# Talking-heads attention and squared-ReLU FFN: pairs of heads transposed at full width, and one stock of PSUM banks

## The chip, the cores and the metric

The kernel runs on one core of one Trainium2 chip. The metric is the device time of one execution in microseconds. TensorE (PE) multiplies matrices into PSUM, which has eight banks; VectorE (DVE) and ScalarE (ACT) read PSUM and write SBUF; GpSimd (POOL) works on SBUF and issues DMAs, SyncE (SP) issues DMAs.

## What is computed

The reference, cut to its core (8 batches, 12 heads, 448 positions, head size 64; the FFN is 768 to 2048 to 768):

```python
scores = scale * np.matmul(q, k.transpose(0, 1, 3, 2))
scores = np.einsum('bhij,hg->bgij', scores, w_pre)
scores = scores - np.max(scores, axis=-1, keepdims=True)
attn = np.exp(scores)
attn = attn / (np.sum(attn, axis=-1, keepdims=True) + 1e-09)
attn = np.einsum('bhij,hg->bgij', attn, w_post)
x = np.matmul(attn, v)            # heads side by side: [8*448, 768]
h = np.maximum(x @ w_in, 0.0)
out = (h * h) @ w_out
```

The heads are mixed before and after the softmax, so all twelve heads of a query row are needed together.

## The kernel before

**Attention, per batch.** q and k of a batch lie in SBUF as bf16, positions in partitions (`qs`, `ks`). For each of the six pairs of heads, `t_qk` transposes both heads' q and k on TensorE into one PSUM bank (a product with the identity `ident` as the moving operand): for each of 4 row groups of q and 4 blocks of k, and for each head of the pair, one product of 64 stationary columns that writes PSUM partitions 0 to 63 or 64 to 127. These are lines L274 (q) and L279 (k), 16 products per pair. Three copies bring the result out: `kt` takes both heads' k in one copy of 128 partitions, `qz` takes each head's q into its own half, with zeros in the other half, so that a score product over 128 partitions gives one head. `qz` and `kt` have 8 slots, so a pair's transposes wait for the last scores of the pair that had the slot before.

`score` (L312) multiplies one head and 112 query rows by 448 keys; an eviction copies it to `snat`, of which there are two. When the 12 heads of a row group are there, DMAs on SyncE's queue (`relayout`, L335) rearrange `snat` into 11 chunks `sch`, each with 10 query rows by 12 heads in 120 partitions. `chunk` then does, 45 times per batch: the mix product m (L365), a minimum on VectorE (L370; signs are turned), the exponential on ScalarE (L373), a reciprocal on VectorE (L379), the second mix's weights on GpSimd (`wq`, L382), four products that transpose and mix at once (L389), and an eviction to `atb`. `av` (L434) multiplies by v with products of 64 columns, evicted on ScalarE (L443) to `xt`.

**FFN.** `unit` works on 128 or 256 positions of a pair of batches: L478 multiplies by the first weights, ScalarE applies the ReLU (L491), GpSimd squares (L494), L510 multiplies by the second weights, VectorE evicts (L525), SyncE stores.

**What sets the order.** TensorE, VectorE, ScalarE and GpSimd run in the order that `Planner.run` writes out. Every operation has an engine (or VectorE and ScalarE, either of them), a cost in ns, a priority (lower goes first, in chunks: chunk c of batch b is 45b + c), the operations that it waits for, and possibly a bank that it takes or gives back. The planner plays time forward; when an engine is idle it takes the most urgent operation that is ready, even one meant for far later. FFN operations have priorities from a million on, so they fill what attention leaves. `copy` is the helper that makes an eviction on VectorE (L233) or ScalarE (L235).

**Banks.** The eight PSUM banks are four pairs with a tag: m for the mix product, a for L389, f for the FFN, g for transposes, scores and av. In the first row group of the first batch scores go round all four tags, and every second transpose of that batch uses f. An operation that needs a bank waits in the plan until its own tag has one free.

**Loads.** The loads of the next batch's q and k are issued by GpSimd at steps 3 and 6 of a batch (18 and 21 in the first), in two groups of three pairs; they wait for that step's `wq` (`gate`) and for the transposes that read the old contents.

Of the kernel before, what the change touches and what calls it, by code (L numbers as in the profile page):

```python
# [23 lines left out]
NR = 4  # L24
PR = S // NR
# [7 lines left out]
NB = 4  # L33
W2B = 2 * S
NSLOT = 8
NE = 5
NSCH = 8
AHEAD = 5
UNITS = [(0, 128), (128, 384), (384, 640), (640, 896)]


# [11 lines left out]
class Planner:  # L53
# [2 lines left out]

    def __init__(self):
        self.ops = []
        self.banks = {}

    def add(self, eng, ns, pri, fn, deps=(), lat=60, bank=None, frees=None):
        op = Op(eng if isinstance(eng, dict) else {eng: ns}, lat, pri, fn, list(deps), bank, frees)
        self.ops.append(op)
        return op

    def run(self):
        order, events, n = [], [], 0
        ready, busy, held = {}, {}, {}
        free = {tag: list(slots) for tag, slots in self.banks.items()}

        def push(op):
            nonlocal n
            for eng in op.engs:
                heapq.heappush(ready.setdefault(eng, []), (op.pri, n, op))
            n += 1

        for op in self.ops:
            for eng in op.engs:
                busy.setdefault(eng, 0)
                ready.setdefault(eng, [])  # L80
            if op.left == 0:
                push(op)
        t = 0
        while True:
            for eng, heap in ready.items():
                if busy[eng] > t:
                    continue
                kept = []
                while heap:
                    item = heapq.heappop(heap)  # L90
                    op = item[2]
                    if op.eng is not None:
                        continue
                    if op.bank is not None and not free[op.bank[0]]:
                        kept.append(item)
                        continue
                    args = []
                    if op.bank is not None:
                        held[op.bank] = free[op.bank[0]].pop(0)
                        args.append(held[op.bank])  # L100
                    if len(op.engs) > 1:
                        args.append(eng)
                    op.eng, op.ns, op.at = eng, op.engs[eng], t
                    order.append((op, args))
                    busy[eng] = t + op.ns
                    heapq.heappush(events, (t + op.ns, n, None))
                    heapq.heappush(events, (t + op.ns + op.lat, n + 1, op))
                    n += 2
                    break
                for item in kept:  # L110
                    heapq.heappush(heap, item)
            if not events:
                break
            t = events[0][0]
            while events and events[0][0] == t:
                op = heapq.heappop(events)[2]
                if op is None:
                    continue
                if op.frees is not None:
                    free[op.frees[0]].append(held.pop(op.frees))  # L120
                for x in op.next:
                    x.left -= 1
                    if x.left == 0:
                        push(x)
        assert len(order) == len(self.ops)
        return order
# [3 lines left out]
def kernel(  # L130
# [11 lines left out]
    nc = tc.nc  # L142
    P = nc.NUM_PARTITIONS

    sb = ctx.enter_context(tc.tile_pool(name="sb", bufs=1))
    ps = ctx.enter_context(tc.tile_pool(name="ps", bufs=1, space=bass.MemoryType.PSUM))

    def many(n, name, shape, dtype):
        return [sb.tile(shape, dtype, name=f"{name}{i}") for i in range(n)]
# [3 lines left out]
    vs = sb.tile([P, H, NB, D], BF16, name="vs")  # L153
    qz = many(NSLOT, "qz", [P, 2, S], BF16)
    kt = many(NSLOT, "kt", [P, S], BF16)
    snat = many(2, "snat", [PR, H, S], BF16)
    sch = many(NSCH, "sch", [KC, S], BF16)
    schl = many(2, "schl", [KC, S], BF16)
# [9 lines left out]
    osb = many(2, "osb", [P, DMODEL], F32)  # L168
    w1 = many(NPAIR, "w1", [P, DFF], BF16)
    w2 = many(FT, "w2", [P, DMODEL], BF16)  # L170
    bank = {tag: [ps.tile([P, 512], F32, name=f"{tag}{i}") for i in range(2)] for tag in "mafg"}

    def load_q(b, h0, h1):
        nc.gpsimd.dma_start(
# [56 lines left out]
    def copy(eng, out_, in_):  # L231
        if eng == "DVE":
            nc.vector.tensor_copy(out=out_, in_=in_)  # L233
        else:
            nc.scalar.copy(out=out_, in_=in_)  # L235

    pl = Planner()
    pl.banks = {tag: bank[tag] for tag in bank}
    add = pl.add
    FILL = 1e6  # L240
    slots = {}
# [1 line left out]
    def keep(key, fn):  # L243
        def go(slot):
            slots[key] = slot
            fn(slot)
        return go
# [15 lines left out]
    av_op, xc_op = {}, {}  # L263
    h_op, sq_op, o_op, st_op = {}, {}, {}, {}

    def t_qk(b, p):
        z, kk = qz[(b * NPAIR + p) % NSLOT], kt[(b * NPAIR + p) % NSLOT]
        key = ("f" if b == 0 and p % 2 else "g", "t", b, p)

        def mms(slot):  # L270
            v_ = slot[:, :].bitcast(BF16).rearrange("p (a c) -> p a c", a=2)
            for r in range(NR):
                for x in range(2):
                    nc.tensor.transpose(  # L274
                        v_[64 * x:64 * x + 64, 0, r * PR:(r + 1) * PR], qs[:, 2 * p + x, r, :], ident[0:PR, 0:PR],
                    )
            for j in range(NB):
                for x in range(2):
                    nc.tensor.transpose(  # L279
                        v_[64 * x:64 * x + 64, 1, j * 128:(j + 1) * 128], ks[:, 2 * p + x, j, :], ident[:, :],  # L280
                    )

        def part():
            return slots[key][:, :].bitcast(BF16).rearrange("p (a c) -> p a c", a=2)

        def out_k(eng):
            copy(eng, kk[:, :], part()[:, 1, 0:S])

        def out_q(x, eng):
            copy(eng, z[64 * x:64 * x + 64, x, :], part()[64 * x:64 * x + 64, 0, 0:S])  # L290

        pri = b * NCHUNK - 19 + 1.5 * p
        old = []
        i = b * NPAIR + p - NSLOT
        if i >= 0:
            old = [score_ops[i // NPAIR, NR - 1, 2 * (i % NPAIR) + x] for x in range(2)]
        mm = add("PE", 780, pri, keep(key, mms), [q_in[b, p // 2], k_in[b, p // 2]] + old, lat=200, bank=key)
        a0 = add({"DVE": 310, "ACT": 440}, 0, pri, out_k, [mm])
        a1 = add({"DVE": 390, "ACT": 440}, 0, pri, lambda eng: out_q(0, eng), [mm])
        a2 = add({"DVE": 390, "ACT": 440}, 0, pri, lambda eng: out_q(1, eng), [mm])  # L300
        add("FREE%d" % len(pl.ops), 0, pri, lambda: None, [a0, a1, a2], frees=key)
        trans[b, p] = (mm, [a0, a1, a2])
# [274 lines left out]
    for b in range(B):  # L577
# [10 lines left out]
        for r in range(NR):  # L588
            for h in range(H):
                score(b, r, h)  # L590
            for c in range(CPR * r, CPR * (r + 1)):
                relayout(b, c)
                chunk(b, c)
                n = n0 + c
                if b == 0 and c in (3, 6, 9):
                    load_w1(2 + c // 3, n, gate(n))
                if b == 0 and len(w2_in) < FT and (c in range(12, 18) or c >= 24):
                    ft = len(w2_in)
                    w2_in.append(load(3.9e5, n, lambda ft=ft: nc.gpsimd.dma_start(
                        out=w2[ft][:, :], in_=moe_w_out[ft * 128:(ft + 1) * 128, 0:DMODEL], max_dma_last_dim=1024,  # L600
                    ), gate(n)))
                if b + 1 < B and c in ((18, 21) if b == 0 else (3, 6)):
                    g0 = 0 if c in (3, 18) else 6
                    wars = [trans[b, p][0] for p in range(g0 // 2, g0 // 2 + 3)]
                    got = [
                        load(7e5, n, lambda b=b, g0=g0: load_q(b + 1, g0, g0 + 6), wars + gate(n)),
                        load(4e5, n, lambda b=b, g0=g0: load_lo(ks, k, b + 1, g0, g0 + 6), wars + gate(n)),
                        load(3e5, n, lambda b=b, g0=g0: load_hi(ks, k, b + 1, g0, g0 + 6), wars + gate(n)),
                    ]
                    both = add("DMA", 0, n, lambda: None, got, lat=0)  # L610
                    later[b + 1, g0] = both
            if r == 1:
                for g in range(3):
                    av(b, 0, g)
                if b > 0:
                    unit(b // 2, 0 if b % 2 == 0 else 2)
# [54 lines left out]
```

## Time and profile before

Three runs took 661.95, 665.9 and 667.5 us, the median is 665.9 us. The profiled execution took 667.06 us, and its span from first to last instruction is 665.3 us.

| | busy us | share of the span |
|---|---|---|
| TensorE products | 618.6 | 93% |
| TensorE weight loads | 444.9 | 67% |
| VectorE | 519.0 | 78% |
| ScalarE | 515.2 | 77% |
| GpSimd | 313.1 | 47% |

Busy time is the union of an engine's instructions. A product's record includes the depth of TensorE's pipeline, which the next product overlaps, so what a product occupies is read from the distance between starts. The granted TensorE clock is 0.969 of full speed over the span. Busy shares are averages over stages with different limits: the start-up (the first 100 us, when weights are loaded as well), six and a half batches of steady work, and an end with the FFN alone.

### The profile page before, as it was taken

The page shows a single profiled execution, that of the slowest core. Times are in us where ns is not written, and L with a number is a line of the kernel's source. Part 1 is how long each engine was busy: PE and PEld are TensorE (multiplying, and loading weights), DVE is VectorE, ACT ScalarE, POOL GpSimd, SP SyncE. Part 2 cuts the span into 40 slices and gives each one's busy share as a digit, 9 for nine tenths or more (in the row PEclk, how much of TensorE's full clock was granted, in tenths as well). Part 3 has the DMA queues.
Part 4 walks back from the last instruction along what each step waited for, and adds up shares of the span by engine and source line. Part 5 has one row for each costly group of instructions (what it writes and reads, how often), then busy time and mean ns, then how long its engine had stood idle before and what let it go on. Part 6 is the DMA issues. An engine that isn't in the chain of part 4 may idle for free.

```text
span 665.3 us, 17942 instructions
## 1 busy us (share of the span) xinstructions
PE 618.6 (93%) x6152; PEld 444.9 (67%) x6152; DVE 519.0 (78%) x1281; ACT 515.2 (77%) x1297; POOL 313.1 (47%) x570
## 2 busy tenths in 40 slices
PE   4778779999998999989999999999999999999996
PEld 2346537766766768766776777775776767777774
DVE  6688687899786897879979798779879798869511
ACT  3578777888876898888887888898888878886520
POOL 7057824723554426732582445552483433453531
PEclk9678889999998999999999999999999999999999
DMA  9899955932294224923296226922387216423011
GB/s 135 146 174 195 185 101 84 180 94 82 76 172 125 64 84 97 194 83 93 87 142 151 86 61 121 192 72 81 109 129 160 86 53 114 141 60 112 6 48 48
DMA packets 100393, 73.53 MB, mean 111 GB/s; under 512 B 18253, under 2 KB 96845, under 8 KB 100301
## 3 DMA queue, kind: packets, MB, share of 16 engines
q0 software_dynamic: 49040, 22.81, 27.6%
q1 hardware_dynamic: 51261, 49.57, 25.8%
q8 instruction: 48, 0.79, 0.5%
q14 instruction: 44, 0.36, 0.1%
HBM read 45.62 MB, written 11.01 MB: 85 GB/s over the span
## 4 chain that ended last, share of the span: by engine, by line
PE 70%; DVE 9%; ACT 7%; DMA 5%; issue 4%; POOL 3%; DVEq 0%; ACTq 0%; SPq 0%; POOLq 0%
PE f L478 19%; PE f L510 18%; PE a L389 10%; PE g L312 9%; PE m L365 8%; PE g L434 5%; DMA sch<-snat 5%; ACT es L373 3%; DVE mn L370 3%; DVE snat L233 2%; ACT qz L235 2%; DVE qz L233 1%; POOL wq L382 1%; DVE kt L233 1%; POOL h L494 1%
## 5 line engine op out<-in xcount | busy, mean ns | idle before, releaser
L382 POOL TENSOR_SCALAR wq<-wback,rc 120x120 bf16<-120x120 f32 x360 | 132.0, 368 | 276.0 <-DVE rc L379 157.9
L373 ACT ACTIVATE es<-m,mn 120x448 bf16<-120x448 f32 x360 | 229.1, 641 | 37.3 <-DVE mn L370 35.1
L370 DVE TENSOR_REDUCE mn<-m 120x1 f32<-120x448 f32 x360 | 213.8, 614 | 10.8 <-PE m L365 9.2
L233 DVE CAST atb<-a 128x480 bf16<-128x480 f32 (+1 forms) x212 | 136.1, 647 | 53.4 <-PE a L389 50.6
L510 PE MATMUL f<-w,h 128*128 128x384 bf16 x896 | 174.9, 326 | 0.0
L478 PE MATMUL f<-xt,w 128*128 128x256 bf16 (+1 forms) x1536 | 165.1, 260 | 0.0
L478 PEld LDWEIGHTS <-w 128*128 128x128 bf16 x1536 | 134.8, 98 | 25.1 <-issue 1.4
L389 PEld LDWEIGHTS <-es 120*128 120x128 bf16 (+1 forms) x1440 | 105.8, 100 | 65.1 <-issue 34.0
L389 PE MATMUL a<-wq,es 120*128 120x120 bf16 (+1 forms) x1440 | 134.8, 220 | 12.2 <-POOL wq L382 11.5
L494 POOL TENSOR_TENSOR h<-hr 128x512 bf16<-128x512 f32 x112 | 116.6, 1042 | 51.8 <-ACT hr L491 46.8
L312 PE MATMUL g<-kt,qz 128*112 128x448 bf16 x375 | 123.6, 366 | 12.5 <-DVE snat L233 8.1
L365 PE MATMUL m<-sch,wmix 120*128 120x448 bf16 x352 | 125.8, 365 | 5.5 <-ACT es L373 4.9
L510 PEld LDWEIGHTS <-h 128*128 128x128 bf16 x896 | 85.5, 98 | 57.4 <-issue 2.3
L235 ACT CAST snat<-g 112x448 bf16<-112x448 f32 x200 | 104.0, 539 | 15.2 <-PE g L312 14.3
L233 DVE CAST snat<-g 112x448 bf16<-112x448 f32 x175 | 106.2, 614 | 9.7 <-issue 3.1
L235 ACT CAST atb<-a 128x480 bf16<-128x480 f32 (+1 forms) x156 | 84.3, 547 | 24.3 <-PE a L389 23.3
L491 ACT ACTIVATE hr<-f 128x512 f32<-128x512 f32 x112 | 66.9, 597 | 24.8 <-PE f L478 22.1
L373 ACT ACTIVATION_READ_ACCUMULATOR es<-m,mn 120x1 f32 x360 | 73.9, 205 | 0.0
L379 DVE RECIPROCAL rc<-sm 120x1 f32<-120x1 f32 x360 | 55.6, 155 | 21.6 <-ACT es L373 16.9
L312 PEld LDWEIGHTS <-qz 128*112 128x112 bf16 x384 | 49.0, 135 | 25.8 <-issue 12.5
L525 DVE COPY osb<-f 128x384 f32<-128x384 f32 x56 | 30.9, 552 | 29.9 <-PE f L510 29.8
L365 PEld LDWEIGHTS <-wmix 120*128 120x128 bf16 x360 | 35.3, 99 | 17.6 <-issue 7.4
(48 smaller groups left out, 324.5 us busy)
## 6 DMA issues: line engine op xcount, KB each, us to landing
sch<-snat SPq DMA_DIRECT2D x352, 105.0 KB
qs<-in_q_dram POOLq DMA_DIRECT2D x14, 336.0 KB, 11.0
vs<-in_v_dram POOLq DMA_DIRECT2D x8, 384.0 KB, 6.0
w<-in_moe_w_in_dram POOLq DMA_DIRECT2D x6, 512.0 KB, 11.1
w<-in_moe_w_out_dram POOLq DMA_DIRECT2D x16, 192.0 KB, 9.6
ks<-in_k_dram POOLq DMA_DIRECT2D x14, 192.0 KB, 11.3
out_dram<-osb SPq DMA_DIRECT2D x7, 330.0 KB
vs<-in_v_dram POOLq DMA_DIRECT2D x8, 288.0 KB, 8.0
```

What stands on the lines that cost most here:

```text
L233: nc.vector.tensor_copy(out=out_, in_=in_)
L235: nc.scalar.copy(out=out_, in_=in_)
L312: nc.tensor.matmul(slot[0:PR, 0:S], lhsT=qz[i][:, x, r * PR:(r + 1) * PR], rhs=kt[i][:, :], start=True, stop=True,)
L365: nc.tensor.matmul(slot[:, 0:S], lhsT=wmix[0:rows, :], rhs=src[0:rows, :], start=True, stop=True,)
L370: nc.vector.tensor_reduce(out=mn[i][0:rows, :], in_=slots[mk][0:rows, 0:S], axis=AX.X, op=ALU.min)
L373: nc.scalar.activation(out=es[i][0:rows, 0:S], in_=slots[mk][0:rows, 0:S], func=ACT.Exp, scale=-1.0, bias=mn[i][0:rows, 0:1], accum_out=sm ...
L382: nc.gpsimd.tensor_scalar(out=wq[i][0:rows, :, 0:ns], in0=wback[0:rows, :, 0:ns], scalar1=rc[i][0:rows, 0:1], scalar2=1.0, op0=ALU.mult, o ...
L389: nc.tensor.matmul(slot[:, jb * H * ns:(jb + 1) * H * ns], lhsT=es[i][0:rows, jb * 128:(jb + 1) * 128], rhs=wq[i][0:rows, :, 0:ns], start= ...
L478: nc.tensor.matmul(slot[:, j * w:(j + 1) * w], lhsT=w1[c2][:, (f0 + j) * 128:(f0 + j + 1) * 128], rhs=xt[:, c2, a:z], start=(c2 == 0), sto ...
L491: nc.scalar.activation(out=hr[gi % 2][:, :], in_=slots[key][:, :], func=ACT.Relu)
L494: nc.gpsimd.tensor_tensor(out=h2_[:, f0:f0 + nf, 0:w], in0=hr[gi % 2][:, :].rearrange("p (f c) -> p f c", f=nf), in1=hr[gi % 2][:, :].rear ...
L510: nc.tensor.matmul(slot[:, 0:384], lhsT=h2_[:, ft, mt * 128:(mt + 1) * 128], rhs=w2[ft][:, nt * 384:(nt + 1) * 384], start=(ft == 0), stop ...
```

## The change

Pairs from batch 1 on: two new copies per pair put both heads' k side by side in `kn` (128 positions by 4 blocks by 2 heads of 64) and both heads' q in `qn` (112 positions by 4 row groups by 2 heads), SBUF to SBUF, on VectorE or ScalarE. The transposes then read these: 4 products of 128 stationary columns for k and 4 for q, which write all 128 partitions, 8 products instead of 16. `kn` and `qn` have two buffers each; a pair's copies wait for the transposes two pairs earlier. The copies' priority is 6 chunks ahead of the transposes', their planned cost is 260 ns on VectorE and 500 on ScalarE, and the planned cost of a pair's transposes goes from 780 to 450. In batch 0 the transposes stay as they were, k now first. The loads of the next batch wait for the copies instead of the transposes.

Banks: all eight are one list, taken from its front and given back to its end. The tags remain as limits: at most 3 for m, 2 for a, 2 for f, 4 for g, and at most 6 for m, a and g together.

```diff
+MOST = {"m": 3, "a": 2, "f": 2, "g": 4, "mix": 6}
...
-        free = {tag: list(slots) for tag, slots in self.banks.items()}
+        free, room = list(self.banks), dict(self.most)
...
-                    if op.bank is not None and not free[op.bank[0]]:
+                    if op.bank is not None and not (
+                        free and room[op.bank[0]] and (room["mix"] or op.bank[0] == "f")
+                    ):
                         kept.append(item)
                         continue
                     args = []
                     if op.bank is not None:
-                        held[op.bank] = free[op.bank[0]].pop(0)
+                        held[op.bank] = free.pop(0)
+                        room[op.bank[0]] -= 1
+                        room["mix"] -= op.bank[0] != "f"
...
                 if op.frees is not None:
-                    free[op.frees[0]].append(held.pop(op.frees))
+                    free.append(held.pop(op.frees))
+                    room[op.frees[0]] += 1
+                    room["mix"] += op.frees[0] != "f"
...
+    qn = many(2, "qn", [PR, NR, 2 * D], BF16)
+    kn = many(2, "kn", [P, NB, 2 * D], BF16)
...
-    bank = {tag: [ps.tile([P, 512], F32, name=f"{tag}{i}") for i in range(2)] for tag in "mafg"}
+    banks = [ps.tile([P, 512], F32, name=f"bank{i}") for i in range(8)]
...
+        i = b * NPAIR + p
+        qp, kp = qn[i % 2], kn[i % 2]
...
+        def pair_up(eng, n_, s_):
+            near(
+                eng, n_[:, :, :].rearrange("p j (x d) -> p j x d", x=2),
+                s_[:, 2 * p:2 * p + 2, :, :].rearrange("p x j d -> p j x d"),
+            )
...
+            for j in range(NB):
+                if b > 0:
+                    nc.tensor.transpose(v_[:, 1, j * 128:(j + 1) * 128], kp[:, j, :], ident[:, :])
+                else:
+                    for x in range(2):
+                        nc.tensor.transpose(
+                            v_[64 * x:64 * x + 64, 1, j * 128:(j + 1) * 128], ks[:, 2 * p + x, j, :], ident[:, :],
+                        )
             for r in range(NR):
-                for x in range(2):
-                    nc.tensor.transpose(
-                        v_[64 * x:64 * x + 64, 0, r * PR:(r + 1) * PR], qs[:, 2 * p + x, r, :], ident[0:PR, 0:PR],
-                    )
-            for j in range(NB):
-                for x in range(2):
-                    nc.tensor.transpose(
-                        v_[64 * x:64 * x + 64, 1, j * 128:(j + 1) * 128], ks[:, 2 * p + x, j, :], ident[:, :],
-                    )
+                if b > 0:
+                    nc.tensor.transpose(v_[:, 0, r * PR:(r + 1) * PR], qp[:, r, :], ident[0:PR, 0:PR])
+                else:
...
-        mm = add("PE", 780, pri, keep(key, mms), [q_in[b, p // 2], k_in[b, p // 2]] + old, lat=200, bank=key)
+        ins = [q_in[b, p // 2], k_in[b, p // 2]]
+        if b > 0:
+            both = {"DVE": 260, "ACT": 500}
+            ins = [
+                add(both, 0, pri - 6, lambda eng: pair_up(eng, kp, ks), [ins[1], t_op.get(i - 2)], lat=80),
+                add(both, 0, pri - 6, lambda eng: pair_up(eng, qp, qs), [ins[0], t_op.get(i - 2)], lat=80),
+            ]
+        mm = add("PE", 450 if b > 0 else 780, pri, keep(key, mms), ins + old, lat=200, bank=key)
+        t_op[i], got_op[b, p] = mm, ins if b > 0 else [mm]
...
-                    wars = [trans[b, p][0] for p in range(g0 // 2, g0 // 2 + 3)]
+                    wars = [op for p in range(g0 // 2, g0 // 2 + 3) for op in got_op[b, p]]
```

`near` calls `copy`. 

More of the change, by code (lines that the diff above doesn't have):

```diff
@@ L58, in __init__ @@
         self.ops = []
-        self.banks = {}
+        self.banks, self.most = [], {}
     def add(self, eng, ns, pri, fn, deps=(), lat=60, bank=None, frees=None):
@@ L237 @@
     pl = Planner()
-    pl.banks = {tag: bank[tag] for tag in bank}
+    pl.banks, pl.most = banks, MOST
     add = pl.add
@@ L264 @@
     h_op, sq_op, o_op, st_op = {}, {}, {}, {}
+    t_op, got_op = {}, {}
     def t_qk(b, p):
@@ L268, in t_qk, with near @@
         key = ("f" if b == 0 and p % 2 else "g", "t", b, p)
+        i = b * NPAIR + p
+        qp, kp = qn[i % 2], kn[i % 2]
+        def near(eng, out_, in_):
+            copy(eng, out_, in_)
+        def pair_up(eng, n_, s_):
[3 more added lines that the diff above has]
+            )
         def mms(slot):
             v_ = slot[:, :].bitcast(BF16).rearrange("p (a c) -> p a c", a=2)
-            for r in range(NR):
-                for x in range(2):
-                    nc.tensor.transpose(
-                        v_[64 * x:64 * x + 64, 0, r * PR:(r + 1) * PR], qs[:, 2 * p + x, r, :], ident[0:PR, 0:PR],
-                    )
-            for j in range(NB):
-                for x in range(2):
-                    nc.tensor.transpose(
-                        v_[64 * x:64 * x + 64, 1, j * 128:(j + 1) * 128], ks[:, 2 * p + x, j, :], ident[:, :],
-                    )
+            for j in range(NB):
[6 more added lines that the diff above has]
+                        )
+            for r in range(NR):
+                if b > 0:
+                    nc.tensor.transpose(v_[:, 0, r * PR:(r + 1) * PR], qp[:, r, :], ident[0:PR, 0:PR])
+                else:
+                    for x in range(2):
+                        nc.tensor.transpose(
+                            v_[64 * x:64 * x + 64, 0, r * PR:(r + 1) * PR], qs[:, 2 * p + x, r, :], ident[0:PR, 0:PR],
+                        )
         def part():
@@ L293, in t_qk @@
         old = []
-        i = b * NPAIR + p - NSLOT
-        if i >= 0:
-            old = [score_ops[i // NPAIR, NR - 1, 2 * (i % NPAIR) + x] for x in range(2)]
-        mm = add("PE", 780, pri, keep(key, mms), [q_in[b, p // 2], k_in[b, p // 2]] + old, lat=200, bank=key)
+        if i >= NSLOT:
+            old = [score_ops[(i - NSLOT) // NPAIR, NR - 1, 2 * ((i - NSLOT) % NPAIR) + x] for x in range(2)]
+        ins = [q_in[b, p // 2], k_in[b, p // 2]]
[7 more added lines that the diff above has]
+        t_op[i], got_op[b, p] = mm, ins if b > 0 else [mm]
         a0 = add({"DVE": 310, "ACT": 440}, 0, pri, out_k, [mm])
```

## The prediction

> **What bounds the kernel now.** I read the page's first part, then busy time by stage, the timeline of TensorE around the transposes, the groups by line with their idle time, and the waits.
>
> ```profile
> PE 618.6 (93%) x6152; PEld 444.9 (67%) x6152; DVE 519.0 (78%) x1281; ACT 515.2 (77%) x1297; POOL 313.1 (47%) x570
> ...
> PE 70%; DVE 9%; ACT 7%; DMA 5%; issue 4%; POOL 3%; DVEq 0%; ACTq 0%; SPq 0%; POOLq 0%
> ```
>
> TensorE is busy 93% of the span and holds 70% of the chain that ended last. An average over stages can mislead, so the next view splits the span (columns: window, length, then busy us and instructions of PE, PEld, DVE, ACT, POOL, granted clock, DMA share, GB/s).
>
> ```profile
> 40.00:100.00 60.00, 45.72 (x453) 29.31 (x452) 47.63 (x120) 48.18 (x122) 34.50 (x62) 0.87 1.01 167
> ...
> 320.00:395.00 75.00, 74.34 (x779) 55.75 (x777) 64.95 (x161) 66.30 (x170) 39.85 (x71) 1.00 0.50 111
> ...
> 545.00:600.00 55.00, 55.00 (x561) 41.15 (x559) 45.54 (x112) 47.02 (x120) 25.18 (x47) 1.00 0.42 105
> ```
>
> ```profile
> 100.00:600.00 500.00, 488.93 (x5036) 359.37 (x5035) 417.64 (x1028) 424.69 (x1079) 239.02 (x441) 0.99 0.50 109
> ```
>
> From 100 to 600 us TensorE idles 11.1 us of 500: what is taken off it here shortens the run, as long as VectorE (84%) and ScalarE (85%) keep up. From 40 to 100 us it idles 14.3 us of 60, the DMA engines are full (1.01) and the chain of that stretch runs mostly over VectorE and ScalarE: a TensorE saving there is worth little.
>
> **The transposes, before.** The timeline of TensorE shows what one group (16 products of 64 rows of output) occupies. Columns: start, length of the merged piece, engine, line, operation, tiles, form, count. Starts count, since the last 0.2 us of each length is pipeline depth that the next instruction overlaps.
>
> ```profile
> 300.16 0.36 PE L365 MATMUL m<-sch,wmix 120*128 120x448 bf16 x1
> 300.46 0.39 PE L274 MATMUL g<-ident,qs 112*64 112x112 bf16 x8
> 300.68 0.39 PE L279 MATMUL g<-ident,ks 128*64 128x128 bf16 x8
> 301.00 0.38 PE L389 MATMUL a<-wq,es 120*128 120x120 bf16 x4
> 301.22 0.33 PE L510 MATMUL f<-w,h 128*128 128x384 bf16 x1
> ```
>
> ```profile
> 302.07 0.35 PE L312 MATMUL g<-kt,qz 128*112 128x448 bf16 x1
> 302.27 0.35 PE L365 MATMUL m<-sch,wmix 120*128 120x448 bf16 x1
> ```
>
> ```profile
> 142.55 0.39 PE L274 MATMUL g<-ident,qs 112*64 112x112 bf16 x8
> 142.77 0.39 PE L279 MATMUL g<-ident,ks 128*64 128x128 bf16 x8
> 142.99 0.45 PE L434 MATMUL g<-atb,vs 128*64 128x220 bf16 x6
> ```
>
> Three readings. First, a 448-column product holds TensorE 0.20 us (302.07 to 302.27), but 0.30 us when a transpose group follows (300.16 to 300.46): 0.10 us to enter. Second, eight q transposes take 0.22 us, 27 ns each, for 112 columns: a rate of about 4 columns per ns, where the 4 products of L389 take 0.22 us for 480 columns, about 2.2 per ns. So two half-width products already run side by side, and joining them into full ones saves almost no streaming. Third, the eight k transposes take 0.32 us until a full-width product starts, but 0.22 us until the half-width L434 starts: 0.10 us to leave. The group costs 0.10 + 0.22 + 0.32 = 0.64 us, of which 0.20 us is entering and leaving.
>
> **The transposes, after.** From batch 1 on, 4 products of 128 columns and 4 of 112, full width. The chain shows 12 L478 products of 256 columns in 1.31 us, 2.35 columns per ns; 960 columns then take 0.41 us, with nothing to enter or leave. Saved per group: 0.64 - 0.41 = 0.23 us. Ends: at L389's rate the 8 products take 0.44 us (saves 0.20); if each had to wait for its own weight load, 98 ns in the L478 row, 0.78 us (loses 0.14). L389 issues four load-and-product pairs in 0.22 us, so I take 0.23. The window from 100 to 600 us holds 288 k products, 36 groups: 36 x 0.23 = **-8.3 us**. Batch 1's six groups lie before 100 us and count as nothing (at most -1.4).
>
> One rule speaks against this. The Trainium skill, "TensorE: Matmul & The Clock Gate", section "Back-to-back issue gap", puts a sustained stream of load-and-product pairs at about 81 ns for 128 columns. By it the eight products would take an estimated 0.65 us and the term would be zero; the L389 row with its 55 ns disagrees, and the row decides.
>
> **The copies.** Each of 42 pairs gets two copies, 84 of 128 x 512 or 112 x 512 bf16 from SBUF to SBUF, on whichever of VectorE and ScalarE the planner finds free. No row before shows such a copy.
>
> ```profile
> L491 ACT ACTIVATE hr<-f 128x512 f32<-128x512 f32 x112 | 66.9, 597 | 24.8 <-PE f L478 22.1 <-POOL wq L382 2.1 <-POOL h L494 0.2
> ...
> L233 DVE COPY qz<-g 64x448 bf16<-64x448 bf16 x52 | 20.1, 387 | 9.3 <-ACT qz L235 7.2 <-ACT kt L235 1.2
> L235 ACT COPY qz<-g 64x448 bf16<-64x448 bf16 x38 | 20.0, 527 | 14.7 <-DVE kt L233 11.9 <-DVE qz L233 1.9 <-PE m L365 0.4
> ```
>
> On VectorE the lower end is a one-element SBUF operation, the reciprocal's 0.155 us; the upper is the f32 cast of 480 elements, 0.65 us, scaled to 512: 0.70. I take the nearest row, 0.387 x 512/448 = 0.44. On ScalarE 0.53 (same type, 448) to 0.65; I take the 512-element row, 0.60. The helper's rows give VectorE 385 and ScalarE 347 copies in the window, so 44 copies go to VectorE (19 us) and 40 to ScalarE (24 us); six sevenths lie between 100 and 600 us: 16.6 and 20.6. The idle 82 and 75 us there hide them, but the shares become 434/492 = 88% and 445/492 = 91%. The copies' priorities are more urgent than the chunks in flight, so minima (L370), exponentials (L373) and evictions queue behind them, and TensorE's L389 waits for those through L382. I price this as a doubling of what L389 now waits for L382 in the window: **+3.1 us** (0 to +24, below). For batch 1 the copies stand in the stretch whose chain runs over VectorE and ScalarE: 12 copies of 0.52 us on two engines are 3.1 us; half of it on the path, **+1.5** (0 to 3.1).
>
> A second rule says they could be dearer. The Trainium skill, "SBUF — State Buffer", section "Who interferes with whom", says that a VectorE copy in a two-port mode and a GpSimd instruction exclude each other for their whole length. No run here shows it. If it holds, an estimate from its statement with GpSimd busy 48% and half of 0.37 to 1.04 us left would add some 7 us to VectorE.
>
> **The bank stock.** Before, every kind of work owns two banks. After, any six of eight may serve scores, mixes, attention and transposes (up to 4, 3 and 2), and f keeps two.
>
> ```profile
> L389 PE MATMUL a<-wq,es 120*128 120x120 bf16 (+1 forms) x1200 | 109.3, 216 | 3.5 <-POOL wq L382 3.1
> L365 PE MATMUL m<-sch,wmix 120*128 120x448 bf16 x294 | 101.9, 355 | 0.8 <-ACT es L373 0.8
> L312 PE MATMUL g<-kt,qz 128*112 128x448 bf16 x316 | 100.4, 354 | 6.3 <-DVE snat L233 4.3 <-ACT snat L235 1.1 <-DVE qz L233 0.4
> ```
>
> Waits for an eviction are bank waits: 0.8 + 6.3 = 7.1 us from 100 to 600, less about 4 us at two places where the eviction itself waited for a relayout transfer (one wait of 2.7 us near 204 us): about 3. From 40 to 100 us, L365 waits 3.2 and L312 4.6 us so; a third of 7.8 may reach the end there, since other limits stand close. Together **-5.6 us** (0 to -11). The loss side: four scores at once put two more evictions of 0.54 to 0.61 us ahead of a minimum; paid once for each of 28 row blocks at half of 0.58 us it would be +8. The filler products hide it in the plan; I take nothing.
>
> **Loads.** The next batch's q and k loads on GpSimd's queue now wait for the pair copies instead of the transposes. They are issued at steps 3 and 6 of a batch, behind their gate on L382, when all six pairs have long been transposed: nothing. No DMA and no SyncE issue is added; behind a pair copy whose load came late, VectorE's or ScalarE's chunk work would stand, and the loads land before the first transposes by 0.5 to 4 us today.
>
> **Sum.** -8.3 + 3.1 + 1.5 - 5.6 = -9.3 us. The profiled execution took 667.06 us (span 665.3 and 1.8 around it): 657.8. The median, 665.9, is 1.2 lower: 656.6. I forecast **657.5 us**.
>
> **Rivals.** (1) *VectorE and ScalarE become the pace* (ends slower). They need 88% and 91%, both together 89%; the densest stage today, 320 to 395 us, shows 66.30/75 = 88% on ScalarE. If ScalarE can't hold more than between its mean and that best, 0.868, the stretch lasts 445/0.868 = 513 us instead of 500: +13, with +1.5 and -5.6: 676. It decides from the point where less than 0.89 can be held (445/500). For it: a fixed order can't shift a late eviction, and the planner's prices (440 for a ScalarE copy that takes 530) are below the rows. Against: TensorE is 99% busy in that densest stage, so 88% starved nothing. Chance 0.21.
> (2) *The saving turns into waits*: TensorE gets through sooner and L389 and L312 wait that much longer for the same evictions; -8.3 + 8.3 and the banks' small part leave 662 to 669, say 665. For it: the exposed waits already sit on L382 and snat. Chance 0.27.
> (3) *The stock gives more than I price*: all bank waits go, start-up gains too (-11), copies hidden: 667 - 8.3 - 11 = 648. Chance 0.15.
> (4) *The copies and products don't change TensorE* (weight loads bind): no saving, +3.1 + 1.5 - 5.6: 666; inside rival 2's chance.
> The forecast itself has 0.37.
>
> **How the numbers follow.** About 1% is what a measurement of this kernel can tell from no change (661.95 to 667.5 in three runs): 659.2 and 672.6. Faster: 0.37 and 0.15, 0.52. Within: 0.27. Slower: 0.21. The range reaches from below rival 3 to rival 1: 642 to 676; the forecast's own is 650 to 663.
>
> **What would show it.** Right: TensorE groups of 8 products with 4 k starts in 0.22 us, 0.20 us from a 448-column product to the group, none of L274's 64-wide forms after batch 0; about 84 new copy rows between SBUF tiles near 0.44 and 0.60 us; less idle at L312 and L365. Wrong: L389's wait for L382 grown beyond 10 us, ScalarE above 90% with TensorE idle beside it, or products spaced near 0.1 us.

## The result, and the profile after

The changed kernel takes 675.22 us (median; 673.92 to 675.67) against 664.81 us: a ratio of 1.0146, 95% interval 1.0116 to 1.0175. It is slower by 1.5%, where 657.5 us had been forecast. The profiled execution took 675.67 us, its span is 673.9 us.

The page's first part and its chain, of the changed kernel:

```profile
PE 610.9 (91%) x5816; PEld 444.1 (66%) x5816; DVE 521.1 (77%) x1326; ACT 530.9 (79%) x1336; POOL 313.0 (46%) x570
...
PE 63%; DMA 14%; ACT 8%; DVE 8%; issue 4%; POOL 2%; DVEq 0%; ACTq 0%; SPq 0%; POOLq 0%
PE bank L514 17%; PE bank L546 17%; DMA sch<-snat 12%; PE bank L425 9%; PE bank L348 7%; PE bank L401 7%; PE bank L470 5%; ACT es L409 3%; DVE mn L406 2%; ACT snat L244 2%; POOL wq L418 1%; DVE snat L242 1%; DVE atb L242 1%; ACT qz L244 1%; DVE qz L242 1%
```

Two subtractions split the change of the span. TensorE's busy time fell from 618.6 to 610.9 us, by 7.7. Its idle time, the span less that, rose from 46.7 to 63.0 us, by 16.3. The sum, +8.6, is the change of the span. The 7.7 is not the transposes' saving alone: `e2` below, with the transposes of before, shows 610.5 us busy, and `e1`, with the full-width ones, 619.9, since a product counts as busy for longer while the granted clock is low (see the last section). And what holds the chain in TensorE's place is the relayout, `sch<-snat`: 12% of it now, 5% before.

By stage (columns as in the prediction):

```profile
40.00:100.00 60.00, 47.91 (x455) 32.21 (x453) 54.19 (x136) 53.13 (x137) 35.09 (x64) 0.85 0.97 161
...
320.00:395.00 75.00, 71.24 (x696) 53.46 (x694) 63.30 (x161) 64.99 (x166) 37.08 (x67) 0.98 0.51 115
...
545.00:600.00 55.00, 54.65 (x584) 41.20 (x582) 47.44 (x120) 48.54 (x127) 27.20 (x52) 1.00 0.43 108
```

```profile
100.00:600.00 500.00, 471.90 (x4630) 348.24 (x4630) 428.21 (x1088) 436.75 (x1112) 234.45 (x441) 0.99 0.50 110
```

From 100 to 600 us TensorE idles 28.1 us instead of 11.1. At the same time attention runs ahead: the last mix product starts 603 us after the span's start, 622 before, and FFN work alone fills a longer end. So the loss is not that attention came late. TensorE stood during attention, and the FFN products that could have filled the holes stood elsewhere in its order.

Where it stood, in the groups of the same window:

```profile
L425 PE MATMUL bank<-wq,es 120*128 120x120 bf16 x1227 | 110.7, 217 | 7.9 <-POOL wq L418 5.3 <-ACT snat L244 2.0
L401 PE MATMUL bank<-sch,wmix 120*128 120x448 bf16 x301 | 104.2, 357 | 13.4 <-DMA sch<-snat 9.7 <-DVE snat L242 2.7 <-DVE mn L406 0.9
L348 PE MATMUL bank<-kt,qz 128*112 128x448 bf16 x312 | 102.7, 356 | 5.0 <-DVE snat L242 4.8 <-DVE atb L242 0.2
```

L401 is the mix product (L365 before), L348 the score (L312), L425 was L389. The mix product's idle time went from 0.8 to 13.4 us, and 9.7 of that ended with the landing of a relayout, which held up no mix product in this window before. The relayout held up evictions too: `snat` has two buffers, so the evictions of a row group wait until the relayouts of two groups before have landed. VectorE's, before and after:

```profile
L233 DVE CAST snat<-g 112x448 bf16<-112x448 f32 x175 | 106.2, 614 | 9.7 <-issue 3.1 <-DMA sch<-snat 3.1 <-PE g L312 2.3
```

```profile
L242 DVE CAST snat<-bank 112x448 bf16<-112x448 f32 x191 | 114.5, 613 | 21.0 <-DMA sch<-snat 17.2 <-PE bank L348 2.0 <-issue 1.0
```

With ScalarE's, evictions waited 23.1 us for relayouts over the run, 3.1 before. TensorE's longest wait, 4.78 us of L348 for such an eviction, stands behind one of them (5.1 us).

One place shows a mix product's wait, first in the chain of waits, then in SyncE's queue (start, length):

```profile
325.79 6.59 DMA sch<-snat
332.38 0.05 issue
332.43 0.36 PE bank L401
...
336.41 7.76 DMA sch<-snat
344.17 0.05 issue
344.22 0.36 PE bank L401
```

```profile
325.79 3.42 SPq L371 DMA_DIRECT2D sch<-snat  x4
329.26 0.70 SPq L374 DMA_DIRECT2D schl<-snat  x1
330.06 0.80 SPq L371 DMA_DIRECT2D sch<-snat  x1
330.95 3.38 SPq L596 DMA_DIRECT2D out_dram<-osb  x4
335.29 10.67 SPq L371 DMA_DIRECT2D sch<-snat  x10
```

These relayouts landed 6.59 and 7.76 us after their issue. The plan counts 770 + 400 + 3800 ns, 4.97 us. In between, four output stores hold SyncE's queue for 3.4 us; the next relayout is issued 0.96 us after them. In the plan a row group's first mix product may start as soon as its relayout lands there. Over the 28 row groups of batches 1 to 7, the time from the first relayout's issue to the first mix product has a median of 10.1 us and a minimum of 8.0 before; after, 7.4 and 4.7, with 12 of 28 under 7 us. The 4.7 shows that some relayouts do land as early as the plan has it.

### The profile page after: what moved, and what is told of

Same layout as the page of the kernel before. It is cut to its first block, busy times and chain, and to the rows that moved or that the text cites. A ratio compares the mean times of both kernels' runs of the same rounds, so it can differ in the third digit from the quotient of the medians.

```text
span 673.9 us, 17320 instructions
## 1 busy us (share of the span) xinstructions
PE 610.9 (91%) x5816; PEld 444.1 (66%) x5816; DVE 521.1 (77%) x1326; ACT 530.9 (79%) x1336; POOL 313.0 (46%) x570
## 4 chain that ended last, share of the span: by engine, by line
PE 63%; DMA 14%; ACT 8%; DVE 8%; issue 4%; POOL 2%; DVEq 0%; ACTq 0%; SPq 0%; POOLq 0%
PE bank L514 17%; PE bank L546 17%; DMA sch<-snat 12%; PE bank L425 9%; PE bank L348 7%; PE bank L401 7%; PE bank L470 5%; ACT es L409 3%; DVE mn L406 2%; ACT snat L244 2%; POOL wq L418 1%; DVE snat L242 1%; DVE atb L242 1%; ACT qz L244 1%; DVE qz L242 1%
## 5 line engine op out<-in xcount | busy, mean ns | idle before, releaser
L418 POOL TENSOR_SCALAR wq<-wback,rc 120x120 bf16<-120x120 f32 x360 | 131.0, 366 | 268.7 <-DVE rc L415 163.0
L409 ACT ACTIVATE es<-bank,mn 120x448 bf16<-120x448 f32 x360 | 229.4, 643 | 29.2 <-DVE mn L406 21.2
L406 DVE TENSOR_REDUCE mn<-bank 120x1 f32<-120x448 f32 x360 | 212.8, 611 | 11.2 <-PE bank L401 10.3
L546 PE MATMUL bank<-w,h 128*128 128x384 bf16 x896 | 174.1, 327 | 1.6 <-ACT snat L244 1.4
L514 PE MATMUL bank<-xt,w 128*128 128x256 bf16 (+1 forms) x1536 | 165.6, 262 | 0.3 <-ACT qz L244 0.3
L514 PEld LDWEIGHTS <-w 128*128 128x128 bf16 x1536 | 136.1, 99 | 27.8 <-issue 6.5
L425 PE MATMUL bank<-wq,es 120*128 120x120 bf16 (+1 forms) x1440 | 132.7, 220 | 21.2 <-POOL wq L418 17.4
L425 PEld LDWEIGHTS <-es 120*128 120x128 bf16 (+1 forms) x1440 | 105.4, 100 | 69.7 <-issue 33.9
L530 POOL TENSOR_TENSOR h<-hr 128x512 bf16<-128x512 f32 x112 | 116.4, 1039 | 74.0 <-ACT hr L527 73.1
L242 DVE CAST atb<-bank 128x480 bf16<-128x480 f32 (+1 forms) x196 | 123.4, 639 | 33.9 <-PE bank L425 32.2
L401 PE MATMUL bank<-sch,wmix 120*128 120x448 bf16 x352 | 124.3, 368 | 18.7 <-DMA sch<-snat 14.7
L348 PE MATMUL bank<-kt,qz 128*112 128x448 bf16 x384 | 130.0, 376 | 7.6 <-DVE snat L242 4.8
L242 DVE CAST snat<-bank 112x448 bf16<-112x448 f32 x191 | 114.5, 613 | 21.0 <-DMA sch<-snat 17.2
L244 ACT CAST atb<-bank 128x480 bf16<-128x480 f32 (+1 forms) x172 | 94.8, 558 | 16.3 <-PE bank L425 14.4
L244 ACT CAST snat<-bank 112x448 bf16<-112x448 f32 x193 | 98.9, 543 | 8.8 <-DMA sch<-snat 3.8
L348 PEld LDWEIGHTS <-qz 128*112 128x112 bf16 x384 | 50.9, 138 | 19.6 <-ACT qz L244 4.2
L401 PEld LDWEIGHTS <-wmix 120*128 120x128 bf16 x360 | 35.4, 100 | 30.0 <-DMA sch<-snat 17.4
## 6 DMA issues: line engine op xcount, KB each, us to landing
qs<-in_q_dram POOLq DMA_DIRECT2D x14, 336.0 KB, 11.1
```

The lines of the kernel that those rows point to most:

```text
L348: nc.tensor.matmul(slot[0:PR, 0:S], lhsT=qz[i][:, x, r * PR:(r + 1) * PR], rhs=kt[i][:, :], start=True, stop=True,)
L401: nc.tensor.matmul(slot[:, 0:S], lhsT=wmix[0:rows, :], rhs=src[0:rows, :], start=True, stop=True,)
L406: nc.vector.tensor_reduce(out=mn[i][0:rows, :], in_=slots[mk][0:rows, 0:S], axis=AX.X, op=ALU.min)
L409: nc.scalar.activation(out=es[i][0:rows, 0:S], in_=slots[mk][0:rows, 0:S], func=ACT.Exp, scale=-1.0, bias=mn[i][0:rows, 0:1], accum_out=sm ...
L418: nc.gpsimd.tensor_scalar(out=wq[i][0:rows, :, 0:ns], in0=wback[0:rows, :, 0:ns], scalar1=rc[i][0:rows, 0:1], scalar2=1.0, op0=ALU.mult, o ...
L425: nc.tensor.matmul(slot[:, jb * H * ns:(jb + 1) * H * ns], lhsT=es[i][0:rows, jb * 128:(jb + 1) * 128], rhs=wq[i][0:rows, :, 0:ns], start= ...
```

## The experiments

All times are medians, and each kernel ran with the kernel before on the same chip (664.5 to 665.8 us). "Products" means the pair copies with the full-width transposes.

**The parts apart.** `e1`: the products, with the old four pairs of banks. `e2`: the stock, with the old transposes. `e3`: the change with

```diff
-MOST = {"m": 3, "a": 2, "f": 2, "g": 4, "mix": 6}
+MOST = {"m": 2, "a": 2, "f": 2, "g": 2, "mix": 6}
```

> The pair copies and full-width transposes, with the four pairs of banks of before. Theory A (the bank stock lets the plan run attention denser than relayouts and evictions follow, TensorE then stands, and FFN products are left for the end): the transposes' 8 us stay saved, 654 to 662 us, attention ends within 5 us of before (620 us), TensorE idle from 100 to 600 us under 15 us. Theory B (the 84 copies load VectorE and ScalarE so that attention comes late): 670 to 680 us, as slow as after. Theory C (the transposes' lower price in the plan, 450 for 780, alone makes the plan too dense): 666 to 674.

> The bank stock with its limits 3, 2, 2, 4 and 6, with the transposes of before and no copies. Theory A: slower than before, 672 to 685 us, attention ends 10 us or more earlier than before's 620 us, TensorE idle from 100 to 600 us above 22 us. Theory B: the stock helps or does nothing, 658 to 667 us.

> The changed kernel with limits of 2 for each of m, a, f and g: one stock that rotates through eight banks, but no kind of work holds more than before. Theory A (it is the looser limits): 654 to 663 us, like the products alone. If the rotation itself does the harm (more banks' readers to wait for): 672 us or more. Theory B: 670 to 680 us.

Measured: e1 675.38 us (1.0147, 1.0119 to 1.0175), e2 665.98 (1.0015, 0.9997 to 1.0033), e3 672.21 (1.0099, 1.0072 to 1.0126). Theory A, with which I went in, fell at all three: the stock alone costs nothing that is clear of noise, the products alone cost as much as the whole change, and tight limits don't repair it. Theory B's numbers held at all three, and e3 also lies in the range given for the rotation (672 or more). B's mechanism, attention that comes late, shows only where the limits are tight: the last mix product starts at 640 us in e1 and 633 in e3, against 622 before and 603 in the changed kernel. Half of A was right to look at: e2's last mix product starts at 577 us, 45 us earlier than before, and the time doesn't improve, since TensorE stands more within attention (idle 54.2 us) and FFN is left for the end.

**The landing price.** `e4` is the changed kernel with one thing of the plan moved, a relayout's landing; the instructions do the same work in another order.

```diff
-lat=5500 if b == 0 and c else 3800      # relayout; the last chunk's likewise
+lat=7500 if b == 0 and c else 6500
```

> The changed kernel, with the plan told that a relayout lands 6.5 us (7.5 in batch 0) after its issue instead of 3.8 (5.5); nothing else differs. Theory A in the form that the plan's too early landing is what makes TensorE stand: TensorE's waits for relayouts (14.7 us in the changed kernel) fall below 4 us and the time to 657 to 668 us. If the landing price is not the cause: 672 to 678 us.

Measured: 642.56 us, ratio 0.9661 (0.9636 to 0.9686): 33 us off the changed kernel, 22 us better than the kernel before, and far outside the expected range. In the window from 100 to 600 us, stage view and then TensorE's waits (total, times, longest):

```profile
100.00:600.00 500.00, 493.95 (x4916) 368.38 (x4911) 438.59 (x1116) 446.87 (x1133) 246.68 (x459) 1.00 0.51 111
```

```profile
PE bank L401 <- DMA sch<-snat: 2.7, 5, 0.8
PE bank L425 <- POOL wq L418: 2.2, 7, 0.5
```

TensorE idles 6.0 us there instead of 28.1; its waits for relayouts fell from 9.7 to 2.7 us, and the time from relayout to first mix has a median of 8.7 us. ScalarE holds 446.87/500 = 89% and VectorE 88% in it. Over the whole run TensorE's waits for relayouts fell from 14.7 to 8.4 us, not below 4 as theory A had it; the evictions' waits for relayouts fell from 23.1 to 0.2.

The same price in the other corners: `e5` before, `e6` the products on the old banks, `e9` the stock.

> The kernel before, with the plan told the later landing of a relayout (6.5 and 7.5 us for 3.8 and 5.5), nothing else. Theory D (the too early landing hurts whatever the change; the change itself is worth its 8 us of TensorE under an honest plan): 646 to 654 us, so that the changed kernel with the same landing (642.6) is 4 to 11 us faster than this. Rival E (the cure works only together with the stock's spare banks): 660 to 667 us. Rival F (the later landing gains its 30 us here too or more): 632 to 643.

> Pair copies and full-width transposes with the old four pairs of banks, and the later landing in the plan. Theory D: 8 us under the kernel before with the later landing, 638 to 648 us. Rival E: 665 to 675 us, as without the later landing. Rival B (the copies' load on VectorE and ScalarE): slower than the kernel before with the later landing by 5 us or more.

> The bank stock alone (transposes of before, no copies), with the later landing in the plan. It fills the fourth corner beside 656.7 (neither), 666.3 (products alone) and 642.6 (both). If the gain of the later landing comes with the stock and the products add their 8 us of TensorE: 647 to 654 us. If the copies cost here as much as on the old banks (10 us): 628 to 638 us. If the stock needs the products for its gain: 655 to 665 us.

| landing in the plan | neither | stock | products | both |
|---|---|---|---|---|
| 3.8 us | 664.5 | 666.0 | 675.4 | 675.2 |
| 6.5 us | 656.7 | 658.6 | 666.3 | 642.6 |

Three corners gain 7 to 9 us and the changed kernel 33. Theory D's numbers for e5 and e6 were missed (expected 646 to 654 and 638 to 648), and rival E holds in part: the large gain needs stock and products together. e5 lies in none of its three ranges; e6 meets rival E's range and also rival B's condition (9.6 us slower than e5); e9 meets its third case. What the other corners gain doesn't come from mix products that wait less for relayouts: the kernel before has no such wait, and with the stock it only goes from 6.3 to 5.3 us in the window. e6 also shows a new wait that the prediction had named and priced at nothing, a pair copy that stands at the head of ScalarE's and VectorE's queue until its load lands (window from 195 to 215 us):

```profile
ACT kn L238 <- DMA ks<-in_k_dram: 3.3, 1, 3.3
PEld L291 <- ACT kn L238: 3.0, 1, 3.0
PE g L291 <- ACT kn L238: 2.7, 1, 2.7
DVE kn L236 <- DMA ks<-in_k_dram: 2.0, 1, 2.0
```

**What the width itself is worth.** Three kernels keep the copies and put 16 half-width products back, which read the halves of `qn` and `kn`:

```diff
-nc.tensor.transpose(v_[:, 1, j * 128:(j + 1) * 128], kp[:, j, :], ident[:, :])
+for x in range(2):
+    nc.tensor.transpose(v_[64 * x:64 * x + 64, 1, j * 128:(j + 1) * 128],
+                        kp[:, j, 64 * x:64 * x + 64], ident[:, :])   # q likewise
```

`e7` does so on the old banks at the old price of 780. `e10` and `e11` keep the price 450, so the order of every engine is exactly that of e1 and of e4; only TensorE's work differs. `e8` is the changed kernel with the price 780.

> The pair copies without the full-width products: 16 half-width products read the halves of qn and kn, planned at 780 as before, old banks. The transposes' saving is absent, everything else of the products part is there. Rival B (the copies' load or their place in VectorE's and ScalarE's order costs about 18 us): 676 to 688 us. Theory C (the plan's lower price for the products is what hurts): 662 to 669 us.

> The changed kernel whole, with the plan's price for a pair's transposes left at 780 instead of 450. Theory C: 655 to 666 us. If the price is not it: 670 to 679 us.

> The order of every engine exactly as in the run with the products on the old banks (675.4 us), but 16 half-width products that read the halves of qn and kn in place of the 8 full ones; TensorE has 8 us more to do in the same order. If that order is paced by relayouts and evictions, so that TensorE's saving turns into waiting (rival 2 of the prediction): 674 to 678 us, the same within 3 us. If TensorE paces it: 681 to 686 us.

> The order of every engine exactly as in the changed kernel with the later landing (642.6 us), with 16 half-width products in place of the 8 full ones. If under this plan TensorE paces the run, the full-width products are worth their 8 us: 649 to 653 us. If the saving turns into waits here too: 641 to 645 us.

Measured: e7 675.32, e8 671.03, e10 679.15, e11 647.11 us. With the order held fixed, the full width is worth 679.15 - 675.38 = 3.8 us and 647.11 - 642.56 = 4.6 us: about half of the 9 us that the trace shows it saves (0.22 us for each of 42 pairs; the forecast counted 36), in either plan, and neither expectation held. (The four runs of each kernel spread over 2.2 to 3.1 us. The kernel before took 664.5 us beside e10 and e11, 664.7 beside e1 and e4.) Where the other half went in e4 against e11: TensorE's busy time is 7.4 us less (598.6 for 606.0), its idle time 2.5 us more (42.2 for 39.7), at equal clocks (0.980 and 0.979). In e1 against e10 idle time is equal (54.7 and 54.9) and the clock differs, e1 first:

```profile
core 0: 674.6 us, clock 0.958
```

```profile
core 0: 677.3 us, clock 0.970
```

That is these two executions only. Over four runs each, the granted clock is 0.958 to 0.967 in e1 and 0.964 to 0.970 in e10, and at 0.965 they took 675.12 and 679.48 us; so the clock doesn't account for the medians, and where the other half went there stays open.

e7 lies between its two ranges, 0.7 us under rival B's, and e8 in the range for "the price is not it": theory C fell. e7 against before (10.8 us) shows that the price 450 isn't needed for the loss. That e8 lies 4.2 us under the changed kernel doesn't show that the price took part: the last experiments move the time by more with 10 ns.

**More honest prices.** `e12` adds to e4 the profiled durations of VectorE's and ScalarE's work.

> The changed kernel with the later landing and with VectorE's and ScalarE's prices in the plan set to what the profiles show (evictions 614 and 539 for 540 and 440, minimum 614 for 540, exponential with its read-out 847 for 626, reciprocal 155 for 75, pair copies 284 and 630 for 260 and 500, and so on). If all too low prices do the same harm as the landing: 625 to 638 us. If the landing alone mattered: 640 to 646 us. If the lower prices only kept the plan dense in a useful way: 648 or more.

Measured: 664.57 us, 22 us slower than e4, the third case (648 or more). TensorE's wait for the second mix's weights is what grew, in the window from 100 to 600 us to

```profile
PE bank L425 <- POOL wq L418: 16.8, 35, 1.2
```

from 2.2 us in e4. No mix product waited for a relayout in that window, and evictions did so for 0.2 us: an order without these waits is not yet a fast one. A plan with truer prices on two engines is not the better one: with longer prices the plan issues the products and their inputs in another interleaving, and I can't say from these runs why this one waits.

**How much an order is worth.** By then the corners didn't add up. So the last six runs move one price a little: a pair's transposes by 10 ns in the kernel before (`p1`: 770, `p2`: 790) and in the changed one (`p3`: 440, `p4`: 460), and the landing of e4 by 0.2 us (`p5`, `p6`).

> The kernel before with one price in the plan moved by 10 ns (a pair's transposes 770 for 780): nothing of the work, the banks or the copies differs, only the order that the planner writes out. Theory T (the loss is systematic: copies, banks and their place in the plan): 662 to 668 us, within 3 us of before. Theory S (the written-out order is so sensitive that any change to the plan moves the time by several us either way): more than 5 us off, 655 to 660 or 670 to 680.

> The kernel before with the same price at 790. Theory T: 662 to 668 us. Theory S: more than 5 us off in at least one of the two.

> The changed kernel with a pair's transposes at 440 in the plan for 450. Theory T: 672 to 678 us. Theory S: more than 5 us off 675.

> The changed kernel with a pair's transposes at 460 in the plan. Theory T: 672 to 678 us. Theory S: more than 5 us off 675 in at least one of the two.

> The changed kernel with the later landing at 6.3 us (from batch 1 on all relayouts, and batch 0's first row) in place of 6.5. If the later landing cures by its mechanism (a row's first mixes no longer reach TensorE ahead of their relayout): 640 to 650 us. If 642.6 was a lucky order: 655 us or more in this one or the next.

> The same with 6.7 us. If the cure is the mechanism: 640 to 650 us. If a lucky order: 655 us or more in this one or the one before.

| | price - | as it is | price + |
|---|---|---|---|
| before, 780 -/+ 10 ns | 664.4 | 665.3 | 661.2 |
| changed, 450 -/+ 10 ns | 659.5 | 675.2 | 668.9 |
| changed, landing 6.5 -/+ 0.2 us | 647.5 | 642.6 | 646.2 |

The changed kernel at 440 is faster than the kernel before (0.9919, 0.9894 to 0.9944): the same work in another order, 15.7 us under the changed kernel. At 460 it is slower (1.0045, 1.0018 to 1.0072). So theory S holds for the changed kernel, and 675 us is the bad end of a family from 659.5 to 675.2. The kernel before moves by 4.1 us: theory T's range holds at 770, and at 790 neither theory's does (0.8 us under T's). The later landing is no lucky order among its neighbours, which lie within 5 us; beside e12's prices its gain is gone.

The mix products' waits don't tell the three orders of the changed kernel apart. At 440, 450 and 460 they waited 8.7, 9.7 and 9.3 us for relayouts in the window from 100 to 600 us, and 11, 12 and 11 of 28 row groups came under 7 us. The evictions' waits for relayouts differ more, 7.2, 19.5 and 18.4 us; but e8 has 6.2 and takes 671 us, so no single wait explains the times.

## Why the prediction was wrong, by its steps

- **The transposes' 8.3 us: right, as TensorE's work.** A group in the changed kernel:

```profile
362.15 0.35 PE L348 MATMUL bank<-kt,qz 128*112 128x448 bf16 x1
362.34 0.38 PE L297 MATMUL bank<-ident,kn 128*128 128x128 bf16 x4
362.56 0.36 PE L305 MATMUL bank<-ident,qn 112*128 112x112 bf16 x4
362.76 0.35 PE L401 MATMUL bank<-sch,wmix 120*128 120x448 bf16 x1
```

  It takes 0.42 us from its first start to the next instruction, and the score before it holds TensorE 0.19 us: nothing to enter or leave (0.41 was predicted, 0.64 measured before). The 81 ns a product that the Trainium skill gives ("TensorE: Matmul & The Clock Gate", section "Back-to-back issue gap") would make it an estimated 0.65 us; these rows show 53 ns a product.
- **"What is taken off it here shortens the run": the step that failed.** It rested on TensorE's 98% busy. But the order of all four engines is fixed, and TensorE is that busy only because the plan put an FFN product wherever it expected a wait. What the change alters is the whole written-out order, and a new order has new waits: 16.3 us more idle time, twice the saving. With the order held fixed, 3.8 and 4.6 us of some 9 arrive. That the order and not the work makes the loss is shown by `p3`: the same work in another order takes 659.5 us. The half that arrives was within rival 2's idea; that a reordered plan can lose more than the change saves was in none of my cases.
- **The bank stock's -5.6 us: wrong.** Alone it measured +1.3 us, not clear of noise. In the changed kernel L348's idle time fell only from 6.3 to 5.0, of which 4.8 is the one wait behind a relayout, and the mix products that could now come earlier met relayouts still under way: 13.4 us at L401, which the prediction's row had at 0.8. e2 has this wait as well, 6.3 us for relayouts. The wait that takes the place of the one removed was asked for evictions only. Before, no mix product waited for a relayout, and so I didn't price it; evictions did, and the prediction set some 4 us of TensorE's waits behind such evictions aside as if they would stay the same; the evictions' own wait for relayouts grew from 3.1 to 23.1 us.
- **The copies, +4.6 us: prices near, effect not settled.** The wait that the +3.1 was a doubling of, L389's for L382 (3.1 us), is 5.3 after (L425 for L418): about as priced. 48 copies went to VectorE and 36 to ScalarE (44 and 40 predicted):

```profile
L244 ACT COPY kn<-ks 128x512 bf16<-128x512 bf16 x20 | 12.4, 634 | 0.0
...
L242 DVE COPY qn<-qs 112x512 bf16<-112x512 bf16 x26 | 9.2, 358 | 0.1
L242 DVE COPY kn<-ks 128x512 bf16<-128x512 bf16 x22 | 8.7, 397 | 0.1
```

  0.63 us on ScalarE (0.60 predicted), 0.38 on VectorE (0.44). Alone on the old banks they go with +10.8 us (e7), and with +9.6 under the later landing together with the full width (e6 against e5). On the old banks e1, e7 and e6 all lie about 10 us up, and their last mix product starts 10 to 18 us later than without copies, which speaks for the copies there. With the stock p3 lies 6.5 us under e2 and e4 16 us under e9, copies and all. Each of these is one order, in a family where 10 ns move up to 16 us, so how much of it is the copies' load stays open.
- **Rival 1 gave 676 us for a reason that is not there.** ScalarE was to fail above 0.868; in e4 it holds 0.89 with TensorE 99% busy and the time is 642.6 us. A rival's number that fits is no evidence for the rival.
- **Loads, "nothing": right for the changed kernel**, where no pair copy waited for a load; on the old banks one did in e1 (2.6 us) and six in e6 (three on ScalarE, 7.0 us; three on VectorE, 3.3).

What the runs settle: in the changed kernel the loss goes with the written-out order and not with the work, and a later landing in the plan makes the changed kernel 18 to 22 us faster than the kernel before, in three neighbouring orders. What stays open: which waits make up the 10 us, why products and stock gain so much more from that together than apart, and which part of the +10 on the old banks belongs to the copies.

## What to carry to other kernels

Where a planner writes the order out, a change to any price or resource rewrites all of it: price the change's own work from the trace, then ask what the new order will wait for, and measure two or three neighbours (a price moved by 1 to 3%) before believing a single time. Compare the plan's latencies with the trace first; here moving one of them, a DMA's landing at 5.0 us in the plan and 6.6 and 7.8 in the two places shown, took 33 us off the changed kernel and 7 to 9 off the others. But truer prices are no cure by themselves: with two engines' prices corrected as well (e12), the gain was lost again. An engine that is 98% busy in a fixed order is not thereby the bound: put the saved work back in the same order to see how much of it arrives.

## What the runs showed of the hardware

**A VectorE copy can stand behind a GpSimd instruction.** Of 48 copies from SBUF to SBUF on VectorE 39 took 0.27 to 0.30 us, three 0.35, and six 0.53 to 1.92. Each of these six starts while a GpSimd instruction runs. One of them (VectorE, then GpSimd):

```profile
432.08 1.07 DVE L242 COPY kn<-ks 128x512 bf16<-128x512 bf16 x1
```

```profile
431.96 1.04 POOL L530 TENSOR_TENSOR h<-hr 128x512 bf16<-128x512 f32 x1 [0.27 <-ACT hr L527]
```

The copy ends 0.15 us after the square does, and so do all seven that began beside a square (L530). This agrees with the rule of the Trainium skill ("SBUF — State Buffer", section "Who interferes with whom") that of a VectorE instruction in a two-port mode and a GpSimd instruction whichever issues first has the shared ports for its whole length, and the other waits. The cost is some 4 us on VectorE over the run: the mean is 0.376 us, the median 0.283, and (0.376 - 0.283) x 48 = 4.5. Not every GpSimd instruction did this: two copies that began just behind the start of a `wq` (L418) took 0.28 and 0.30 us.

**A wait of a few us can cost a second time.** Around the end of TensorE's longest wait, 4.78 us up to 425.10 us, the granted clock (after POOL's column) is 0.63 and then 0.52 of full speed:

```profile
422.00:426.00 4.00, 0.90 (x7) 0.68 (x7) 1.58 (x4) 0.00 (x0) 0.36 (x1) 0.63 0.45 143
426.00:430.00 4.00, 4.00 (x37) 3.56 (x36) 2.54 (x8) 1.57 (x3) 1.74 (x3) 0.52 0.37 105
430.00:434.00 4.00, 4.00 (x64) 3.56 (x62) 3.72 (x11) 3.31 (x10) 1.91 (x4) 1.00 0.28 81
```

In the four us from 426 TensorE is busy throughout, at half speed: the 24 products of L514 that start at 425.42 take 2.56 us until the next instruction starts, where 24 of the same form at full clock took 1.34 (229.52 to 230.86). If the clock was either half or full, the rows put the half at about 423.0 to 429.8, an estimate. It doesn't follow every such wait: after one of 3.03 us, up to 500.1, the rows from 498 to 506 show 1.00.
